# Retention with a state scaled by position: keys on ScalarE, one state sum a tile, gate columns summed by fours

## The chip, the cores and the metric

The kernel runs on one core of one Trainium2 chip. Time is device time in microseconds (us), one execution from start to end. Its engines work side by side, each in the order of its own queue, and wait for each other by semaphores: TensorE (PE, matrix multiplication into PSUM; PEld is its weight load), VectorE (DVE), ScalarE (ACT), GpSimd (POOL), and SyncE (SP), whose queue here starts most DMA transfers.

## The reference, cut to what matters

Three layers in float32: a retention layer, a mixture of experts over its tokens, and a dense MLP with a gated activation. The change touches the first one and the routing columns that are computed from it.

```python
# q, k, v: (8 batches, 8 heads, 576 positions, 64)
gamma = 1.0 - 2.0 ** (-5.0 - np.arange(H))              # one decay for each head
rel = pos[:, None] - pos[None, :]
Dmat = np.where(rel >= 0, gamma[:, None, None] ** rel, 0.0)
ret = (q @ k.T / 8) * Dmat                              # no softmax
x = ret @ v                                             # (4608 tokens, 512)
skip_score = x @ w_skip; logits = x @ w_gate            # 9 columns for the routing
```

## The kernel before

The 4608 tokens are 36 tiles of 128, and nine tiles (`PER`) hold two batches: the tiles tau = 0 to 3 and the first half of tau = 4 are one batch, the second half of tau = 4 and tau = 5 to 8 the other. The kernel has three phases: `phase_a` (retention, routing, and in its gaps the splitting of later weights into two parts), `phase_b` (experts), `phase_c` (the MLP). All instructions are issued in the order in which the Python code calls them; there is no planner. `phase_a` takes the first 244 us, and the change lies in it alone.

Retention goes tile by tile with a running state. For tile t:

- `load` brings q and k (turned, so that the head dimension is on the partitions) and k and v (natural), 1 MB, by SP's queue. The transfer for tile t + 4 goes to the memory of tile t and waits until `mix2(t)` has read it.
- `scores(t)` multiplies k and q of the tile (L403, pairs of heads on two halves of the PE rows), and DVE multiplies the result by the decay matrix into `ret` (L410). Scores have two PSUM buffers, and so has `ret` in SBUF.
- `scale(t)`: POOL multiplies q by gamma^i (`qp`, L384); DVE multiplies k by gamma^(128 - i) (`kp`, L390).
- `state(t)`: 8 matmuls of `kp` and v (L423) give the tile's 64 x 64 state for each head, in the one PSUM buffer `stp`.
- `decay(t)`: POOL multiplies the old state by gamma^128 (`old`, L432). `state_out(t)`: DVE adds the product and `stp` (L444), or copies at a batch's first tile (L442). There are two instructions, for the partition halves, since the state `st` is stored as 128 x 128 blocks for two heads each, with zeros off the diagonal.
- `mix1(t)`: 4 matmuls of `st` of tile t - 1 and `qp` (L458). `mix2(t)`: 8 matmuls of v and `ret` into the same PSUM (L466). ACT copies the sum out as `xT` (L470).
- `rows(t)` turns `xT` back (L480), ACT copies (L482), SP stores. `gate_mm(t)` multiplies `xT` by the nine routing columns in four column groups of PE (L493), ACT copies the result (L496). `gate_turn(t)` turns that (L501), and DVE sums the four parts out of PSUM (L502).

In pass t of the loop the order is: `load(t + 4)`, `state(t)`, `state_out(t)`, `scale(t + 1)`, `decay(t + 1)`, `scores(t + 1)`, `gate_turn(t - 2)`, `mix(t)`, routing of a finished group of four tiles (`route1`, in the next pass `rank`, `slots`, `gates`: some 20 short DVE instructions), `rows(t - 1)`, `gate_mm(t - 1)`, then, in three of four passes, one step of the weight conversion (`conv_step`: L205 to L243, on ACT, DVE and SP). From pass 16 on, an expert weight is split in some passes (L156 on ACT, L159 on DVE). A PE instruction that waits holds up all that is behind it on PE, and so on each engine.

`gate_turn(t - 2)` takes its PSUM from the tag `stp`, which has one buffer and is also that of `state`. So the turn waits until `state_out(t)` has read `stp`, and `state(t + 1)` waits until L502 has read the turned columns. The PSUM tags are `s1` (two buffers of two banks) and `pg`, `stp`, `xT`, `pr` (one bank each).

Of the kernel before, what the change touches and what calls it, by code (L numbers as in the profile page):

```python
# [8 lines left out]
F32 = mybir.dt.float32  # L9
# [10 lines left out]
P = 128  # L20
NT = 36
# [28 lines left out]
C_GQ = C_D + 2 * 1024  # L50
C_GK = C_GQ + 2 * 512
C_GS = C_GK + 8
C_W = C_GS + 4


@with_exitstack
def retention_moe_mlp_kernel(
# [240 lines left out]
    def phase_a():  # L298
        actx = ExitStack()
        with actx:  # L300
# [24 lines left out]
            def dload(eng, off, n):  # L325
# [33 lines left out]
                                    base=0, channel_multiplier=-1)  # L359
            st = [a1.tile([P, KD, P], F32, name=f"st{i}") for i in range(2)]  # L360
            for s in st:
                nc.vector.memset(s, 0.0)
            logits = a1.tile([P, NT, 9], F32, name="logits")
            oh = a1.tile([P, NT + 16, E + 1], BF16, name="oh")
# [10 lines left out]
            qp_t, kp_t, ret_t, xT_t = {}, {}, {}, {}  # L375
            stp = [None, None]

            def scale(t):
                if t >= NT:
                    return  # L380
                tau = t % PER
                if tau != 0:
                    qp = ap.tile([P, 512], F32, tag="qp", name="qp")
                    nc.gpsimd.tensor_tensor(out=qp, in0=in_t[t][:, 0, :],  # L384
                                            in1=dcol(C_GQ + (512 if tau == 4 else 0), 512), op=ALU.mult)
                    qp_t[t] = qp
                if tau != 8:
                    kp = ap.tile([P, E, 64], F32, tag="kp", name="kp")
                    g = dcol(C_GK, 8).unsqueeze(2).to_broadcast([P, E, 64])
                    nc.vector.tensor_tensor(out=kp, in0=in_t[t][:, 2, :].rearrange("p (h d) -> p h d", h=E),  # L390
                                            in1=g, op=ALU.mult)
                    kp_t[t] = kp
# [19 lines left out]

            def state(t):
                tau = t % PER
                if tau == 8:
                    return
                sp = psx.tile([P, KD, 64], F32, tag="stp", name="stp")
                p0 = 64 if tau == 4 else 0
                kp = kp_t.pop(t)
                v = in_t[t][:, 3, :].rearrange("p (h d) -> p h d", h=E)  # L420
                for c in range(KD):
                    for r in range(2):
                        nc.tensor.matmul(out=sp[64 * r:64 * r + 64, c, :], lhsT=kp[p0:, 2 * c + r, :],  # L423
                                         rhs=v[p0:, 2 * c + r, :], start=True, stop=True)
                stp[0] = sp

            def decay(t):

                if t % PER not in (0, 4, 8) and t < NT:
                    g = cst[C_GK][:, 8:12].unsqueeze(2).to_broadcast([P, KD, P])  # L430
                    old = ap.tile([P, KD, P], F32, tag="old", name="old", bufs=1)
                    nc.gpsimd.tensor_tensor(out=old, in0=st[(t - 1) % 2], in1=g, op=ALU.mult)  # L432
                    stp[1] = old

            def state_out(t):
                tau = t % PER
                if tau == 8:
                    return
                for r in range(2):
                    p = slice(64 * r, 64 * r + 64)  # L440
                    if tau in (0, 4):
                        nc.vector.tensor_copy(out=st[t % 2][p, :, p], in_=stp[0][p])  # L442
                    else:
                        nc.vector.tensor_tensor(out=st[t % 2][p, :, p], in0=stp[0][p], in1=stp[1][p, :, p], op=ALU.add)  # L444

# [6 lines left out]
            def mix1(t):  # L452
                tau = t % PER
                x = mix_t[t] = psx.tile([P, KD, P], F32, tag="xT", name="xTp")
                if tau != 0:
                    qp = qp_t.pop(t)
                    for c in range(KD):
                        nc.tensor.matmul(out=x[:, c, :], lhsT=st[(t - 1) % 2][:, c, :],  # L458
                                         rhs=qp[:, c * P:(c + 1) * P], start=c == 0, stop=False)

# [37 lines left out]

            def gate_turn(t, tag="pg", at_once=True):
                pg = psx.tile([P, P], F32, tag=tag, name="pg")  # L500
                nc.tensor.transpose(pg, gs_t.pop(t), ident)  # L501
                add = lambda: nc.vector.tensor_reduce(out=logits[:, t, :],  # L502
                                                      in_=pg.rearrange("p (k c) -> p c k", k=KD)[:, 0:9, :],
# [5 lines left out]
            def route1(ts):  # L509
                t0, n = ts[0], len(ts)  # L510
                sl = slice(t0, t0 + n)
                lg = logits[:, sl, 0:E]
                sh = [P, n, E]
# [8 lines left out]
                eq, am, cm, d = tmp("eq"), tmp("am", [P, n]), tmp("cm", [P, n]), tmp("d")  # L522
                nc.vector.tensor_scalar(out=cm, in0=logits[:, sl, 8], scalar1=0.0, scalar2=None, op0=ALU.is_gt)
                nc.vector.tensor_scalar(out=oh[:, sl, E], in0=cm, scalar1=0.0, scalar2=None, op0=ALU.is_equal)
# [170 lines left out]
            scores(0)  # L695
            for t in range(L):
                if t != 31:
                    load(min(t + 4, 35) if t < 33 else NT)
                if t == 1:
                    conv_load(0)  # L700
                if t == 0:
                    dload(nc.sync, C_D + 1024, 1024)
                    dload(nc.sync, C_GQ + 512, 512)
                if t == 2:
# [16 lines left out]
                scale(t + 1)  # L721
                decay(t + 1)
                scores(t + 1, between=between if ts else None)
# [7 lines left out]
                if t > 1:  # L731
                    gate_turn(t - 2, "stp")
                mix(t)
                slots_e(ts)
                if t - 2 in ends:
                    route1(ends[t - 2])
                    ranks.append(ends[t - 2])
# [11 lines left out]

            pair = GROUPS[-1]  # L750
            gate_turn(L - 3)
            gate_mm(L - 2, "pr")
            scale(L)
            decay(L)
            ret = scores(L, False)
            ts = ranks.pop()
            rank(ts)
            add = gate_turn(L - 2, "stp", False)
            slots(ts)
# [433 lines left out]
def tables():  # L1193
# [8 lines left out]
    for var, m in enumerate((dm, dm * blk[None])):  # L1202

        out[:, C_D + 1024 * var:C_D + 1024 * (var + 1)] = m.reshape(4, 2, P, P).transpose(2, 1, 0, 3).reshape(P, 1024)
    gq = (g[:, None] ** i[None, :]) / 8.0
    for var, m in enumerate((gq, gq * (i < 64)[None])):

        out[:, C_GQ + 512 * var:C_GQ + 512 * (var + 1)] = np.repeat(m.reshape(4, 2, P).transpose(1, 0, 2).reshape(2, 512), 64, 0)
    out[:, C_GK:C_GK + 8] = g[None, :] ** (128.0 - i[:, None])
    out[:, C_GS:C_GS + 4] = np.repeat((g ** 128.0).reshape(4, 2).T, 64, 0)  # L1210
    return out.astype(np.float32)
# [19 lines left out]
```

## Time and profile before

| | us |
|---|---|
| median of 3 runs | 1347.86 (1342.99 to 1348.15) |
| the profiled execution | 1347.85 |
| its span, from the first to the last instruction | 1346.1 |
| share of the span in which PE, DVE, ACT, POOL are busy | 95%, 42%, 30%, 29% |
| mean granted TensorE clock | 0.983 of full speed |

The busy shares of the whole span are those of a PE-bound kernel, but they are means over three phases. The change lies in the first 244 us, so the stretch that counts is that of the loop over the tiles, from 28 to 222 us, which holds 30 tiles. Most of what follows is read in it.

### The profile page before, as it was taken

To read this page: it belongs to the slowest core of one execution; us is meant where nothing else is said; L and a number is where in the kernel's file an instruction comes from. 1 tells how busy PE (TensorE), PEld (TensorE's weight loads), DVE (VectorE), ACT (ScalarE), POOL (GpSimd) and SP (SyncE) were. 2 spreads that over 40 slices of the span, in tenths; PEclk is the share of its full clock that TensorE was granted. 3 is DMA by queue.
4 is the path that set the end of the run, shared out by engine and by line. 5 is a ranking of instruction groups with operands and counts; after the bars stand their busy time and mean duration, and the time that the engine had idled before them with its cause. 6 is when DMAs were issued, how large, how long until landed. Compare 5 with 4: busy or idle time off the path is not lost.

```text
span 1346.1 us, 19306 instructions
## 1 busy us (share of the span) xinstructions
PE 1278.6 (95%) x7682; PEld 1058.3 (79%) x7682; DVE 570.9 (42%) x1037; ACT 410.4 (30%) x708; POOL 386.6 (29%) x332
## 2 busy tenths in 40 slices
PE   8887888899999999999999999999999999999995
PEld 6676666788888888788888888888888888888884
DVE  5988888477887873641111111111111111111111
ACT  2223322444444442332222222222222222222221
POOL 4556445313223221122232222232222222222221
PEclk9989889999999999999999999999999999999998
DMA  9989884547777798430010000000010000000000
GB/s 362 264 235 312 273 291 158 171 145 227 258 237 244 267 317 338 174 102 32 1 44 27 24 32 16 17 32 24 9 39 24 32 16 17 32 0 0 32 0 33
DMA packets 59806, 163.53 MB, mean 121 GB/s; under 512 B 9492, under 2 KB 12564, under 8 KB 53824
## 3 DMA queue, kind: packets, MB, share of 16 engines
q1 hardware_dynamic: 52160, 146.38, 32.6%
q0 software_dynamic: 6592, 15.01, 3.4%
q8 instruction: 62, 1.02, 0.3%
q10 hardware_dynamic: 960, 0.86, 0.2%
q14 instruction: 32, 0.26, 0.1%
HBM read 121.47 MB, written 41.52 MB: 121 GB/s over the span
## 4 chain that ended last, share of the span: by engine, by line
PE 75%; DVE 12%; issue 6%; DMA 4%; POOL 1%; ACT 1%; another core or an unknown queue 0%; POOLq 0%; ACTq 0%; DVEq 0%
PE o L1078 29%; PE ch L1053 27%; PE y L904 6%; PE h L887 5%; DVE ret L410 2%; DMA xd<-xr,ent 1%; PE eh L272 1%; PE cpt L1042 1%; DMA xr<-xd,ent 1%; DVE st L444 1%; PE xTp L466 1%; DVE kp L390 1%; DVE cva L217 1%; PE xTp L458 1%; PE s L403 1%
## 5 line engine op out<-in xcount | busy, mean ns | idle before, releaser
L1053 PE MATMUL ch<-cx,w 128*128 128x512 f32 (+1 forms) x1728 | 398.0, 379 | 3.0 <-DVE gt L1057 3.0
L1078 PE MATMUL o<-w,gh 128*128 128x512 f32 x1120 | 377.7, 398 | 0.0
L1053 PEld LDWEIGHTS ch<-cx,w 128*128 128x128 f32 x1728 | 312.8, 188 | 70.4 <-DVE gt L1057 4.6
L1064 POOL TENSOR_TENSOR gl<-gt,gh 128x512 fp32r<-128x512 f32 (+1 forms) x144 | 178.6, 1240 | 605.2 <-ACT gh L1063 590.1
L1057 DVE SCALAR_TENSOR_TENSOR gt<-r,ch 128x512 f32<-128x512 f32 (+1 forms) x144 | 94.8, 658 | 592.1 <-ACT r L1055 592.1
L1078 PEld LDWEIGHTS o<-w,gh 128*128 128x128 f32 x1120 | 210.6, 188 | 48.1
L1055 ACT ACTIVATE r<-ch,small 128x512 f32<-128x512 f32 (+1 forms) x144 | 95.8, 665 | 435.2 <-PE ch L1053 435.2
L1078 PE MATMUL o<-w,gl 128*128 128x512 f32 x560 | 221.4, 395 | 0.0
L904 PE MATMUL y<-w,hh 128*112 128x512 f32 x384 | 132.4, 400 | 0.0
L887 PE MATMUL h<-x,w 128*128 128x336 f32 x768 | 128.4, 316 | 0.6 <-ACT x L879 0.6
L887 PEld LDWEIGHTS h<-x,w 128*128 128x128 f32 x768 | 122.5, 188 | 6.8 <-ACT x L879 0.8
L1063 ACT CAST gh<-gt 128x512 fp32r<-128x512 f32 (+1 forms) x144 | 86.2, 598 | 134.0 <-DVE gt L1057 133.2
L1078 PEld LDWEIGHTS o<-w,gl 128*128 128x128 f32 x560 | 105.4, 188 | 23.0
L904 PEld LDWEIGHTS y<-w,hh 128*112 128x112 f32 x384 | 67.6, 176 | 18.5
L911 POOL DMA_INDIRECT xd<-xr,ent x24 | 36.3, 1513 | 151.4 <-DVE xr L909 148.1
L159 DVE TENSOR_TENSOR w<-raw,w 128x1024 fp32r<-128x1024 f32 x64 | 78.9, 1235 | 0.0
L904 PE MATMUL y<-w,hl 128*112 128x512 f32 x192 | 75.7, 395 | 0.0
L156 ACT CAST w<-raw 128x1024 fp32r<-128x1024 f32 x64 | 67.0, 1048 | 15.6 <-DMA raw<-in_w_dram 15.5
L470 ACT COPY xT<-xTp 128x512 f32<-128x512 f32 x36 | 21.1, 587 | 154.3 <-PE xTp L466 139.4
L890 ACT ACTIVATE hh<-h 128x336 fp32r<-128x336 f32 x64 | 28.9, 452 | 109.9 <-PE h L887 103.4
L892 DVE SCALAR_TENSOR_TENSOR hl<-h,hh 128x336 fp32r<-128x336 f32 x64 | 32.4, 506 | 46.5 <-ACT hh L890 46.1
L617 POOL DMA_INDIRECT tab<-idt,posi x36 | 37.6, 1045 | 39.6 <-DVE idt L592 17.0
(168 smaller groups left out, 1207.7 us busy)
## 6 DMA issues: line engine op xcount, KB each, us to landing
in<-in_qkv_dram SPq DMA_DIRECT2D x33, 1024.0 KB
raw<-in_w_dram SPq DMA_DIRECT2D x64, 512.0 KB
w<-wsc SPq DMA_DIRECT2D x13, 1024.0 KB
xd<-row SPq DMA_DIRECT2D x36, 256.0 KB
wsc<-cvh SPq DMA_DIRECT2D x18, 512.0 KB
raw<-in_w_in_dram SPq DMA_DIRECT2D x16, 512.0 KB
raw<-in_w_out_dram SPq DMA_DIRECT2D x16, 512.0 KB
cr<-xd SPq DMA_DIRECT2D x31, 256.0 KB
```

Of the source, the lines that this page charges most:

```text
L156: nc.scalar.copy(out=w_tile(i)[:, 0, :], in_=raw_t[i])
L159: nc.vector.tensor_tensor(out=w_t[i][:, 1, :], in0=raw_t.pop(i), in1=w_t[i][:, 0, :].bitcast(F32), op=ALU.subtract)
L617: own_rows("tab", nc.gpsimd.indirect_dma_start(out=tab, out_offset=bass.IndirectOffsetOnAxis(posi[:, t:t + 1], 0), in_=idt2[:, t, :], in_o ...
L887: nc.tensor.matmul(out=h, lhsT=w_t[8 * e + k][:, lw, f * P:(f + 1) * P], rhs=rx[:, k, :], start=n == 0, stop=n == 11)
L904: nc.tensor.matmul(out=y_t[e][t][0:CT, :], lhsT=lg[:, sl], rhs=w[:, rw, :], start=f == 0 and n == 0, stop=f == 7 and n == 2)
L911: own_rows("xd", nc.gpsimd.indirect_dma_start(out=xd, out_offset=bass.IndirectOffsetOnAxis(ent[:, e, t, 0:1], 0), in_=o, in_offset=None, b ...
L1053: nc.tensor.matmul(out=h, lhsT=w_block(f)(k)[:, lw, :], rhs=rx[:, k, :], start=i == 0, stop=i == 11)
L1055: nc.scalar.activation(out=r, in_=h, func=AF.Relu, scale=1.0 / 6.0, bias=bias_half)
L1057: nc.vector.scalar_tensor_tensor(out=gt, in0=r, scalar=1.0, in1=h, op0=ALU.min, op1=ALU.mult)
L1063: nc.scalar.copy(out=gh[:, 0:n], in_=gt)
L1064: nc.gpsimd.tensor_tensor(out=gl[:, 0:n], in0=gt, in1=gh[:, 0:n].bitcast(F32), op=ALU.subtract)
L1078: nc.tensor.matmul(out=o_t[g][t], lhsT=lg[:, sl], rhs=w[:, rw, :], start=f == 0 and n == 0, stop=f == NF - 1 and n == 2)
```

## The change

The state is no longer decayed from tile to tile. Keys are scaled by gamma^(256 - 128 n - i) with n = tau modulo 4, and queries by gamma^(128 n + i - 256) / 8 with n = 1 to 4, so that the powers that belong to the distance of tiles are in the two scales, and the state is a plain sum: st(t) = stp(t) + st(t - 1).

- The POOL product `old` (L432) is gone, and `decay` with it.
- `st` is stored as [128, 4, 64], without zeros. `state_out` is one DVE instruction over 128 partitions, no longer two over 64.
- `mix1` uses 8 matmuls of 64 rows x 64 columns (one for each head), no longer 4 of 128 x 128 with zeros.
- `kp` is written by ACT, head by head: 8 activations (`Copy` with the head's scale from a column of a table), no longer one DVE multiplication of 512 columns.
- `gate_turn` in the loop uses the tag `pg`, and ACT copies the 36 columns to `lg`. DVE sums them once for four tiles (`gate_add`). The last two tiles keep a sum of their own (`gate_turn_add`).
- For tau = 4, POOL scales half of the columns of `qp` and sets the rest to zero.
- The query table has 4 blocks of 512 columns in place of 2, the key table 32 columns in place of 8. Three of the query blocks are loaded by SP in the passes t = 0, 1, 2, ahead of `load(t + 4)`, and the second decay matrix in pass 2 in place of pass 0.

```diff
--- before.py
+++ after.py
...
@@ -357,10 +356,8 @@
             tri = a1.tile([P, P], BF16, name="tri")
             nc.gpsimd.affine_select(out=tri, in_=ones, pattern=[[1, P]], compare_op=ALU.is_gt, fill=0.0,
                                     base=0, channel_multiplier=-1)
-            st = [a1.tile([P, KD, P], F32, name=f"st{i}") for i in range(2)]
-            for s in st:
-                nc.vector.memset(s, 0.0)
-            logits = a1.tile([P, NT, 9], F32, name="logits")
+            st = [a1.tile([P, KD, 64], F32, name=f"st{i}") for i in range(2)]
+            logits = a1.tile([P, 2 * GT, 9], F32, name="logits")
...
             qp_t, kp_t, ret_t, xT_t = {}, {}, {}, {}
-            stp = [None, None]
+            stp = [None]
+
+            def gq(tau):
+                return C_GQ + 512 * ((tau - 1) % 4)
 
             def scale(t):
                 if t >= NT:
@@ -381,14 +381,18 @@
                 tau = t % PER
                 if tau != 0:
                     qp = ap.tile([P, 512], F32, tag="qp", name="qp")
-                    nc.gpsimd.tensor_tensor(out=qp, in0=in_t[t][:, 0, :],
-                                            in1=dcol(C_GQ + (512 if tau == 4 else 0), 512), op=ALU.mult)
+                    n = 64 if tau == 4 else P
+                    cut = lambda x: x.rearrange("p (c i) -> p c i", c=KD)[:, :, 0:n]
+                    nc.gpsimd.tensor_tensor(out=cut(qp), in0=cut(in_t[t][:, 0, :]), in1=cut(dcol(gq(tau), 512)), op=ALU.mult)
+                    if n < P:
+                        nc.gpsimd.memset(qp.rearrange("p (c i) -> p c i", c=KD)[:, :, n:], 0.0)
                     qp_t[t] = qp
                 if tau != 8:
                     kp = ap.tile([P, E, 64], F32, tag="kp", name="kp")
-                    g = dcol(C_GK, 8).unsqueeze(2).to_broadcast([P, E, 64])
-                    nc.vector.tensor_tensor(out=kp, in0=in_t[t][:, 2, :].rearrange("p (h d) -> p h d", h=E),
-                                            in1=g, op=ALU.mult)
+                    n = 8 * (tau % 4)
+                    for h in range(E):
+                        nc.scalar.activation(out=kp[:, h, :], in_=in_t[t][:, 2, 64 * h:64 * h + 64], func=AF.Copy,
+                                             scale=cst[C_GK][:, n + h:n + h + 1])
                     kp_t[t] = kp
 
             def scores(t, at_once=True, between=None):
@@ -411,37 +415,25 @@
                 return lambda: nc.vector.tensor_tensor(out=ret, in0=s, in1=d, op=ALU.mult)
 
             def state(t):
+
                 tau = t % PER
                 if tau == 8:
                     return
-                sp = psx.tile([P, KD, 64], F32, tag="stp", name="stp")
+                stp[0] = psx.tile([P, KD, 64], F32, tag="stp", name="stp")
                 p0 = 64 if tau == 4 else 0
                 kp = kp_t.pop(t)
                 v = in_t[t][:, 3, :].rearrange("p (h d) -> p h d", h=E)
                 for c in range(KD):
                     for r in range(2):
-                        nc.tensor.matmul(out=sp[64 * r:64 * r + 64, c, :], lhsT=kp[p0:, 2 * c + r, :],
+                        nc.tensor.matmul(out=stp[0][64 * r:64 * r + 64, c, :], lhsT=kp[p0:, 2 * c + r, :],
                                          rhs=v[p0:, 2 * c + r, :], start=True, stop=True)
-                stp[0] = sp
-
-            def decay(t):
-
-                if t % PER not in (0, 4, 8) and t < NT:
-                    g = cst[C_GK][:, 8:12].unsqueeze(2).to_broadcast([P, KD, P])
-                    old = ap.tile([P, KD, P], F32, tag="old", name="old", bufs=1)
-                    nc.gpsimd.tensor_tensor(out=old, in0=st[(t - 1) % 2], in1=g, op=ALU.mult)
-                    stp[1] = old
 
             def state_out(t):
                 tau = t % PER
-                if tau == 8:
-                    return
-                for r in range(2):
-                    p = slice(64 * r, 64 * r + 64)
-                    if tau in (0, 4):
-                        nc.vector.tensor_copy(out=st[t % 2][p, :, p], in_=stp[0][p])
-                    else:
-                        nc.vector.tensor_tensor(out=st[t % 2][p, :, p], in0=stp[0][p], in1=stp[1][p, :, p], op=ALU.add)
+                if tau in (0, 4):
+                    nc.vector.tensor_copy(out=st[t % 2], in_=stp[0])
+                elif tau != 8:
+                    nc.vector.tensor_tensor(out=st[t % 2], in0=stp[0], in1=st[(t - 1) % 2], op=ALU.add)
 
             mix_t = {}
 
@@ -455,8 +447,10 @@
                 if tau != 0:
                     qp = qp_t.pop(t)
                     for c in range(KD):
-                        nc.tensor.matmul(out=x[:, c, :], lhsT=st[(t - 1) % 2][:, c, :],
-                                         rhs=qp[:, c * P:(c + 1) * P], start=c == 0, stop=False)
+                        for r in range(2):
+                            p = slice(64 * r, 64 * r + 64)
+                            nc.tensor.matmul(out=x[p, c, :], lhsT=st[(t - 1) % 2][p, c, :],
+                                             rhs=qp[p, c * P:(c + 1) * P], start=c == 0, stop=False)
 
             def mix2(t):
                 tau, x = t % PER, mix_t.pop(t)
@@ -496,10 +490,29 @@
                 nc.scalar.copy(out=gs, in_=pg)
                 gs_t[t] = gs
 
-            def gate_turn(t, tag="pg", at_once=True):
+            lg_t = {}
+
+            def at(t, n):
+                return slice(t % (2 * GT), t % (2 * GT) + n)
+
+            def gate_turn(t):
+
+                pg = psx.tile([P, P], F32, tag="pg", name="pg")
+                nc.tensor.transpose(pg, gs_t.pop(t), ident)
+                g, i = divmod(t, GT)
+                if i == 0:
+                    lg_t[g] = ap.tile([P, GT, KD, 9], F32, tag="lg", name="lg")
+                nc.scalar.copy(out=lg_t[g][:, i], in_=pg.rearrange("p (k c) -> p k c", k=KD)[:, :, 0:9])
+
+            def gate_add(ts):
+                lg = lg_t.pop(ts[0] // GT)[:, 0:len(ts)]
+                nc.vector.tensor_reduce(out=logits[:, at(ts[0], len(ts)), :], in_=lg.rearrange("p t k c -> p t c k"),
+                                        axis=AX.X, op=ALU.add)
+
+            def gate_turn_add(t, tag="pg", at_once=True):
                 pg = psx.tile([P, P], F32, tag=tag, name="pg")
                 nc.tensor.transpose(pg, gs_t.pop(t), ident)
-                add = lambda: nc.vector.tensor_reduce(out=logits[:, t, :],
+                add = lambda: nc.vector.tensor_reduce(out=logits[:, t % (2 * GT), :],
                                                       in_=pg.rearrange("p (k c) -> p c k", k=KD)[:, 0:9, :],
                                                       axis=AX.X, op=ALU.add)
                 return add() if at_once else add
...
@@ -694,13 +707,14 @@
             scale(0)
             scores(0)
             for t in range(L):
+                if t < 3:
+                    dload(nc.sync, gq(t + 2), 512)
+                if t == 2:
+                    dload(nc.sync, C_D + 1024, 1024)
                 if t != 31:
                     load(min(t + 4, 35) if t < 33 else NT)
                 if t == 1:
                     conv_load(0)
-                if t == 0:
-                    dload(nc.sync, C_D + 1024, 1024)
-                    dload(nc.sync, C_GQ + 512, 512)
                 if t == 2:
                     pump_load(1)
                 if t == 3:
...
-                decay(t + 1)
...
                 if t > 1:
-                    gate_turn(t - 2, "stp")
+                    gate_turn(t - 2)
                 mix(t)
                 slots_e(ts)
                 if t - 2 in ends:
+                    gate_add(ends[t - 2])
                     route1(ends[t - 2])
...
-    gq = (g[:, None] ** i[None, :]) / 8.0
-    for var, m in enumerate((gq, gq * (i < 64)[None])):
+    gq = lambda n: g[:, None] ** (128.0 * n + i[None, :] - 256) / 8.0
+    for var, m in enumerate((gq(1), gq(2), gq(3), gq(4))):
 
         out[:, C_GQ + 512 * var:C_GQ + 512 * (var + 1)] = np.repeat(m.reshape(4, 2, P).transpose(1, 0, 2).reshape(2, 512), 64, 0)
-    out[:, C_GK:C_GK + 8] = g[None, :] ** (128.0 - i[:, None])
-    out[:, C_GS:C_GS + 4] = np.repeat((g ** 128.0).reshape(4, 2).T, 64, 0)
+    for n in range(4):
+        out[:, C_GK + 8 * n:C_GK + 8 * n + 8] = g[None, :] ** (256.0 - 128 * n - i[:, None])
     return out.astype(np.float32)
 
 
```

## Rows read from the trace of the kernel before

**Rows 1.** The page: busy time, share of the span and instructions.

```profile
PE 1278.6 (95%) x7682; PEld 1058.3 (79%) x7682; DVE 570.9 (42%) x1037; ACT 410.4 (30%) x708; POOL 386.6 (29%) x332
```

**Rows 2.** Stretches: length, busy time (PE, PEld, DVE, ACT, POOL), clock, DMA share, GB/s.

```profile
15.00:25.00 10.00, 9.55 (x138) 7.85 (x138) 6.10 (x9) 2.61 (x6) 5.53 (x9) 1.00 1.03 419
...
100.00:125.00 25.00, 20.12 (x276) 15.88 (x275) 22.48 (x47) 7.38 (x17) 13.09 (x12) 1.00 0.96 327
...
28.00:222.00 194.00, 161.39 (x2066) 129.25 (x2062) 173.71 (x366) 56.89 (x123) 103.33 (x83) 0.93 0.85 269
```

**Rows 3.** Waits of PE from 28 to 222 us: total, times, longest.

```profile
PE pg L501 <- DVE st L444: 18.3, 11, 3.3
PE pk L565 <- DVE cum L533: 4.2, 4, 1.5
PE pg L501 <- DVE st L442: 3.5, 3, 2.5
...
PE stp L423 <- DVE logits L502: 1.9, 4, 1.0
```

**Rows 4.** Timeline of PE, one tile in which it hardly waits: start, length.

```profile
147.11 0.69 PE L423 MATMUL stp<-in,kp 128*64 128x64 f32 x16
147.73 1.16 PE L403 MATMUL s<-in 64*128 64x128 f32 x16
148.92 0.30 PE L501 MATMUL pg<-ident,gs 128*128 128x128 f32 x1
149.05 1.06 PE L458 MATMUL xTp<-qp,st 128*128 128x128 f32 x8
150.04 1.09 PE L466 MATMUL xTp<-ret,in 128*64 128x128 f32 x16
151.06 0.66 PE L480 MATMUL pr<-ident,xT 128*128 128x128 f32 x4
...
152.01 0.28 PE L423 MATMUL stp<-in,kp 128*64 128x64 f32 x2
```

**Rows 5.** Timeline of PE, a tile in which it waits.

```profile
136.04 0.30 PE L501 MATMUL pg<-ident,gs 128*128 128x128 f32 x1 [2.79 <-DVE st L444]
...
137.16 1.97 PE L466 MATMUL xTp<-ret,in 128*64 128x128 f32 x16
```

**Rows 6.** Timeline of DVE at the same place.

```profile
131.45 1.76 DVE L217 SCALAR_TENSOR_TENSOR cva<-cvb,cva 128x512 f32<-128x512 f32 x1
...
135.05 0.85 DVE L444 TENSOR_TENSOR st<-stp,old 64x256 f32<-64x256 f32 x2
```

**Rows 7.** DVE's groups by line, 28 to 222 us: count, busy us, mean ns.

```profile
L410 DVE TENSOR_TENSOR ret<-s,cst 128x1024 f32<-128x1024 f32 x30 | 36.5, 1217 | 2.6 <-PE xTp L466 1.7 <-PE s L403 0.3
L390 DVE TENSOR_TENSOR kp<-in,cst 128x512 f32<-128x512 f32 x27 | 18.8, 695 | 0.8
L444 DVE TENSOR_TENSOR st<-stp,old 64x256 f32<-64x256 f32 x42 | 17.6, 419 | 7.0 <-PE stp L423 6.7
...
L442 DVE COPY st<-stp 64x256 f32<-64x256 f32 x14 | 5.9, 419 | 3.3 <-PE stp L423 3.2
...
L502 DVE TENSOR_REDUCE logits<-pg 128x9 f32<-128x36 f32 x30 | 5.6, 185 | 0.0
```

**Rows 8.** ACT's groups by line, whole span, those near the new ones.

```profile
L1055 ACT ACTIVATE r<-ch,small 128x512 f32<-128x512 f32 x128 | 88.3, 690 | 425.7 <-PE ch L1053 425.7
...
L205 ACT ACTIVATE cvb<-raw 128x512 f32<-128x512 f32 x32 | 21.8, 682 | 3.9 <-DMA raw<-in_w_out_dram 3.1 <-DMA raw<-in_w_in_dram 0.7
...
L1055 ACT ACTIVATE r<-ch,small 128x256 f32<-128x256 f32 x16 | 7.5, 470 | 9.5 <-PE ch L1053 9.5
```

**Rows 9.** POOL's decay product, 28 to 222 us.

```profile
L432 POOL TENSOR_TENSOR old<-st,cst 128x512 f32<-128x512 f32 x21 | 30.6, 1459 | 45.6 <-DVE st L444 28.5 <-DVE st L442 14.1 <-PE s L403 3.0
```

**Rows 10.** The longest wait for a tile's load, from 15 to 232 us.

```profile
POOL qp L384 <- DMA in<-in_qkv_dram: 2.3, 1, 2.3
```

**Rows 11.** Timeline at the start: the first tile's keys.

```profile
8.12 0.69 DVE L390 TENSOR_TENSOR kp<-in,cst 128x512 f32<-128x512 f32 x1 [4.98 <-DMA cst<-in_consts_dram]
```

## What the change does to the time: the prediction

> **What bounds the kernel now.** The page comes first. Over the whole span PE is busy for 1278.6 of 1346.1 us and DVE for 42% [rows 1]: by these means an edit that saves DVE time would be worth nothing. But the change lies in the tile loop, so the stretches come next. From 28 to 222 us, 30 tiles in 194.0 us (6.47 each), PE is busy 161.4 us and DVE 173.7, which is 90%; the clock is 0.93 and DMA's share 0.85 [rows 2]. So in the loop PE idles 32.6 us and DVE is the fullest engine.
>
> Then PE's waits in that stretch. The largest is the gate turn (L501) for DVE's state sum, 18.3 + 3.5 us; the next tile's state waits 1.9 us for the sum of the gate columns, and the rank matmul 4.2 us for the routing counts [rows 3]. One tile in which PE hardly waits shows what PE needs: from state to state 152.01 - 147.11 = 4.90 us [rows 4]. A tile that waits shows why: the turn starts only when the state sum is done [rows 5], and that sum stands in DVE's queue behind the weight conversion that began at 131.45 [rows 6]. After the wait, `mix2` takes 1.97 us in place of 1.09 [rows 4, 5]; that is nearly twice, as at 1.2 in place of 2.4 GHz.
>
> So in this loop PE and DVE hold each other: the turn and the state share one PSUM buffer, PE can't run ahead of DVE's queue, and each burst of DVE work becomes a gap on PE. Phases B and C start when phase A ends; what the loop saves, the kernel saves.
>
> **The change part by part.** The sum is made against the profiled execution, 1347.85 us (span 1346.1), which stands at the median of the runs, 1347.86.
>
> *The turn moves to another PSUM buffer.* It no longer waits for the state sum: -21.8 us [rows 3]. The state no longer waits for L502: -1.9. What is late next? The new buffer is `pg`, which the gate matmuls use: the turn waits for ACT's copy of the previous gate columns, and `gate_mm(t - 1)` for ACT's new copy `lg`. In the undisturbed tile the turn stands at 148.92 and the gate matmuls come behind `rows`, which begin at 151.06 [rows 4]: 2.1 us for a copy of 36 columns, and ACT is busy only 56.9 of 194 us [rows 2]. I book nothing there. PE still needs the state sum, but only for `state(t + 1)` (the one `stp` buffer) and for `mix1(t + 1)`, most of a tile later, and `ret` and the scores have two buffers. `state(t + 1)` starts 4.9 us after `state(t)` [rows 4], so DVE can be some 4 us late without a gap. Some bursts are longer (a conversion step and a routing group in one pass), so I book +2, between 0 and 10.
>
> *DVE's work.* Keys leave: -18.8 us. The state takes one instruction in place of two; the cost doesn't depend on the partitions as far as 64 x 256 shows, so half of 17.6 + 5.9 goes: -11.8. Thirty sums of 36 columns (5.6) become 8 of 144 columns. Between 0.185 us (36 columns) and 1.217 (1024), on a line, that is 0.30 each: 2.4 us. In all DVE falls by 33.8 to 140.0 us, 4.67 a tile [rows 7]. This is below PE's 4.90, so it is not a term of its own: it is what lets the waits above go.
>
> *ACT's work.* No row shows a 64-column activation with a scale from SBUF. The nearest are L1055, with a bias from SBUF: 690 ns at 512 columns, 470 at 256, on a line 305 at 64 [rows 8]. The bounds are the slope alone, 0.055 us, and a whole 512-column one, 0.69. I take 0.305: 8 x 0.305 = 2.44 us a tile, 65.9 in 27 tiles, and the same for 30 `lg` copies, 9.2. ACT comes to 56.9 + 75.1 = 132 us, 4.40 a tile. The Trainium skill (ScalarE: Activation LUTs, section What ACT_TABLE_LOAD costs) has 186 ns + 0.833 ns a column, and 93 more for an operand by pointer; by it this activation is estimated at 332 ns, and ACT at 138 us. The same page's Rules for kernel authors send multiplications to VectorE and not to ScalarE; no row here shows such a multiplication on ACT.
>
> In ACT's queue the eight keys of tile t + 1 stand ahead of `lg`, `xT(t)`, `row` and `gs`. They wait only for a load and an old buffer. PE wants them 4.9 us later, and `xT` is wanted after `mix2`, 151.06 - 147.11 = 3.95 us into the tile [rows 4]; 2.44 us fit. Cover gone, each 0.1 us more for one activation is 0.8 a tile. At the start there is no cover: the first keys took 0.69 us and the first state waited for them [rows 11]: 2.44 - 0.69 = +1.7.
>
> *PE's work.* `mix1` now issues 8 matmuls, 16 instructions in place of 8. It took 150.04 - 149.05 = 0.99 us. Rows with 16 instructions and 128 columns are `mix2`, 1.02 (two column halves), and the scores, 1.19 (two row halves) [rows 4]. The new form is a mixture of both: I take +0.15, in the 27 tiles that have a `mix1` +4.1 us. The bounds are +0.8 us (as `mix2`) and, if nothing overlaps, 16 at 0.124 = 1.98, +26.7.
>
> *The clock.* At a mean of 0.93 [rows 2], with levels of 1 and a half, 14% of 194 us ran at 1.2 GHz; at the full level that work takes 13.6 us less. Low stretches follow PE's gaps, as in [rows 5]. Two thirds of the gaps go, and I take two thirds: -9, between 0 and -13.6.
>
> *Loads.* The loop moves 269 GB/s x 194 us = 52.2 MB. In 174 us that is 300 GB/s. DMA gave 327 from 100 to 125 us at a share of 0.96, and 419 in a stretch of loads alone [rows 2]. Today's longest late load costs 2.3 us [rows 10]. The tables add 512 KB, 1.3 us of DMA at 419 GB/s. On SP they stand ahead of `load(t + 4)` and wait for nothing, but the last ones are needed within about a tile. For late loads and tables I book +5, between 0 and the whole gain.
>
> *POOL.* The decay product, 30.6 us [rows 9], hangs on the state sum and is off PE's path; I book nothing.
>
> The sum: -21.8 - 1.9 + 2 + 1.7 + 4.1 - 9 + 5 = -19.9, so 1328.0 us; the loop would take 5.8 us a tile.
>
> **The rivals.**
>
> *DMA sets the pace.* At 0.85 of 194 us the DMA engines have 165 us of work [rows 2]. If the share can't rise above about 0.90, the loop takes 183 us: 1337. For it: the share was 0.96 from 100 to 125 us, with little left. Against it: in that row DMA carried 327 GB/s, more than the 300 that the forecast needs.
>
> *The small matmuls don't overlap.* Then `mix1` costs +26.7 and not +4.1: 1328.0 + 22.6 - 5 (loads are not late then) = 1345.6, no change. Against it: halves of rows (L403) and halves of columns (L466) overlap today, 16 in 1.02 to 1.19 us; for it: no row has both at once. The Trainium skill (TensorEngine Tiling (Array Packing), section Key Properties) says that a change of tiling mode drains TensorE; `mix1` now stands in a mode of its own between two others. The undisturbed tile already changes form several times and fits into 4.90 us [rows 4]; no run so far shows the cost of one change alone.
>
> *The wait only moves on*: the change doesn't loosen PE from DVE, since `state(t + 1)` still waits for the sum through `stp`. With DVE at 140 us it would return 33.8 us of work, but if bursts and not the mean hold PE, half of the 21.8 comes back, and with it the clock's 9 halves: 1328.0 + 10.9 + 4.5 = 1343.
>
> *ACT becomes the bound, slower.* Keys stand ahead of `xT` in one queue. ACT has 1.90 us a tile now; with `lg` 2.2. It passes today's 6.47 us when an activation costs (6.47 - 2.2) / 8 = 0.53 us. At the farthest row, 0.69 (0.682 for L205) [rows 8], it is 7.7 us a tile: 37 us more in 30 tiles, 1385. Against it: eight times fewer columns than that row.
>
> **How the numbers follow.** My forecast has 0.62; DMA's pace 0.13, the wait that moves on 0.09, the small matmuls 0.11, ACT 0.05. Runs of this kernel spread over 5 us, so 0.5%, 6.7 us, is about what can be told from no change. The forecast and DMA's pace are faster (0.75), and a little over half of the wait that moves on: 0.80. The rest of that and the small matmuls are within: 0.14. ACT and an unnamed mishap: 0.06. The time is 1328. Below it, no late loads, no residual wait and the full clock make -5 - 2 - 4.6: 1316, and a cheaper `mix1` 1313. Above it the range takes in DMA's pace and reaches the wait that moves on: 1343.
>
> **What would show it.** The turn's wait for the state sum should be gone from PE's waits; from 28 us on a tile should take 5.5 to 6.1 us; the clock in the loop should be above 0.95; `mix1` should take 1.0 to 1.2 us; an activation for the keys 0.25 to 0.35 us, and DVE should fall to some 140 us for 30 tiles. The prediction is wrong if waits for `in` or the tables appear on PE, POOL or ACT, if PE waits for ACT's keys before `state`, or if `mix1` comes near 2 us.

## The result, and the profile after

The changed kernel takes 1323.47 us (median of 4 runs, 1320.12 to 1332.19), the kernel before 1346.74 (4 runs). The ratio is 0.9838, interval 0.9810 to 0.9866: 21.8 us faster by this ratio (23.3 by the two medians), where 19.9 were forecast. The profiled execution is the fastest of the four, 1320.12 us, span 1318.3; some 4 us of its distance from before lie behind phase A, where the change touches nothing.

The same stretch as in [rows 2] (columns as there), and then the 30 tiles themselves, from the start of the fourth `ret` on DVE to that of the 34th:

```profile
28.00:222.00 194.00, 178.20 (x2491) 140.48 (x2488) 141.87 (x357) 119.82 (x391) 87.27 (x79) 0.96 0.89 291
```

```profile
21.20:188.08 166.88, 155.53 (x2244) 120.67 (x2244) 120.07 (x269) 108.17 (x361) 74.44 (x71) 0.96 0.97 320
```

A tile takes 166.88 / 30 = 5.56 us; before, the same 30 tiles took 188.11 (6.27). ACT's busy time has doubled and DVE's is down by a quarter. PE is now the fullest engine, busy for 155.53 of 166.88 us (93%), where before it was DVE with 164.82 of 188.11 (88%). DMA's share is 0.97.

PE's waits, beside [rows 3]:

```profile
PE pk L578 <- DVE cum L546: 3.5, 5, 1.5
PE xTp L452 <- POOL qp L386: 2.9, 1, 2.9
PE s L407 <- DMA in<-in_qkv_dram: 2.1, 2, 1.2
PE pk L577 <- ACT row L476: 1.5, 1, 1.5
...
PE pg L501 <- ACT gs L490: 0.8, 2, 0.5
```

The turn's 21.8 us of waits for the state sum have gone. That is what the prediction said one would see, and the experiments show that it was not the reason. An undisturbed tile on PE, beside [rows 4]:

```profile
97.92 0.69 PE L428 MATMUL stp<-in,kp 128*64 128x64 f32 x16
98.54 1.16 PE L407 MATMUL s<-in 64*128 64x128 f32 x16
...
99.63 0.33 PE L501 MATMUL pg<-ident,gs 128*128 128x128 f32 x1
...
99.89 1.09 PE L452 MATMUL xTp<-qp,st 64*64 64x128 f32 x16
...
100.91 1.09 PE L460 MATMUL xTp<-ret,in 128*64 128x128 f32 x16
101.93 0.66 PE L474 MATMUL pr<-ident,xT 128*128 128x128 f32 x4
```

`mix1` with its 16 instructions takes 100.91 - 99.89 = 1.02 us, as `mix2` does (101.93 - 100.91): the halves overlap. ACT's and DVE's new groups, beside [rows 7, 8] (count, busy us, mean ns):

```profile
L394 ACT ACTIVATE kp<-in,cst 128x64 f32<-128x64 f32 x216 | 54.5, 343 | 0.0
...
L505 ACT COPY lg<-pg 128x36 f32<-128x36 f32 x30 | 5.4, 179 | 6.3 <-PE pg L501 5.2 <-remote 0.9
```

```profile
L436 DVE TENSOR_TENSOR st<-stp,st 128x256 f32<-128x256 f32 x21 | 8.8, 420 | 12.2 <-PE stp L428 12.2
```

The state sum over 128 partitions takes the same 0.42 us as one half did [rows 7].

### The profile page after: what moved, and what is told of

Read it like the earlier page. It is cut to its first block, busy times and chain, and to the rows that moved or that the text cites. A ratio compares the mean times of both kernels' runs of the same rounds, so it can differ in the third digit from the quotient of the medians.

```text
span 1318.3 us, 19928 instructions
## 1 busy us (share of the span) xinstructions
PE 1275.8 (97%) x7938; PEld 1051.0 (80%) x7938; DVE 516.8 (39%) x947; ACT 473.0 (36%) x996; POOL 349.6 (27%) x312
## 4 chain that ended last, share of the span: by engine, by line
PE 67%; issue 7%; DMA 5%; DVE 2%; POOL 2%; ACT 0%; POOLq 0%; SPq 0%; DVEq 0%; ACTq 0%
PE o L1091 30%; PE ch L1066 28%; PE y L917 4%; PE h L900 3%; DMA xd<-xr,ent 3%; DMA xr<-xd,ent 1%; PE cpt L1055 1%; PE eh L271 1%; POOL xr L876 1%; POOL xd L924 1%; PE pt L890 0%; DVE cva L208 0%; DMA raw<-in_w_in_dram 0%; DVE xr L922 0%; DMA gse<-ge 0%
## 5 line engine op out<-in xcount | busy, mean ns | idle before, releaser
L1077 POOL TENSOR_TENSOR gl<-gt,gh 128x512 fp32r<-128x512 f32 (+1 forms) x144 | 178.1, 1237 | 605.6 <-ACT gh L1076 600.6
L394 ACT ACTIVATE kp<-in,cst 128x64 f32<-128x64 f32 x256 | 64.6, 342 | 0.0
L386 POOL TENSOR_TENSOR qp<-in,cst 128x512 f32<-128x512 f32 (+1 forms) x32 | 41.2, 1289 | 55.1 <-DMA in<-in_qkv_dram 16.6
L414 DVE TENSOR_TENSOR ret<-s,cst 128x1024 f32<-128x1024 f32 x35 | 42.6, 1217 | 25.9 <-PE s L407 13.7
```

The source lines that it names most:

```text
L394: nc.scalar.activation(out=kp[:, h, :], in_=in_t[t][:, 2, 64 * h:64 * h + 64], func=AF.Copy, scale=cst[C_GK][:, n + h:n + h + 1])
L1077: nc.gpsimd.tensor_tensor(out=gl[:, 0:n], in0=gt, in1=gh[:, 0:n].bitcast(F32), op=ALU.subtract)
```

## The experiments

Gains are given as the ratio to the kernel before, timed on the same chip; the kernel before took 1339 us there for e1 to e8 and 1348 for e9 to e12. A difference between two experiments is a difference of such ratios, and both intervals count in it. The first four take the change apart. Theory A is the prediction's: the PSUM buffer that the turn and the state share ties PE to DVE's queue. Theory B: the amount of DVE's work is what counts.

**e1_turn_alone**: the kernel before with the gate columns as in the changed one.

```diff
-                    gate_turn(t - 2, "stp")
+                    gate_turn(t - 2)
...
+                    gate_add(ends[t - 2])
                     route1(ends[t - 2])
```

> The kernel before with one part of the change: the gate turn in the PSUM tag pg, ACT's copy lg, one sum for four tiles. Keys stay on DVE, the state decays on POOL. Theory A (the shared PSUM buffer ties PE to DVE's queue): PE's 21.8 us of waits of the turn for the state sum mostly go and the kernel gains 8 to 16 us. Theory B (DVE's amount of work is what holds the loop; DVE keeps about 170 of 194 us): no gain, within 4 us.

Ratio 1.0033 (1.0013 to 1.0052): no gain, some 4 us slower. PE's waits from 28 to 222 us:

```profile
PE pk L584 <- DVE cum L552: 13.6, 6, 3.9
PE stp L423 <- DVE kp L390: 7.8, 5, 4.1
PE xTp L458 <- POOL qp L384: 3.2, 1, 3.2
PE pk L583 <- ACT row L482: 1.8, 1, 1.8
```

The turn waits no more, and PE waits instead for two other products of the same DVE queue: the routing counts and the keys, 13.6 + 7.8 us where the turn had 21.8.

**e2_sum_alone**: the changed kernel with the keys on DVE and the gate turn as before.

```diff
-                    for h in range(E):
-                        nc.scalar.activation(out=kp[:, h, :], in_=in_t[t][:, 2, 64 * h:64 * h + 64], func=AF.Copy,
-                                             scale=cst[C_GK][:, n + h:n + h + 1])
+                    g = cst[C_GK][:, n:n + 8].unsqueeze(2).to_broadcast([P, E, 64])
+                    nc.vector.tensor_tensor(out=kp, in0=in_t[t][:, 2, :].rearrange("p (h d) -> p h d", h=E),
+                                            in1=g, op=ALU.mult)
...
-                    gate_turn(t - 2)
+                    gate_turn_add(t - 2, "stp")
...
-                    gate_add(ends[t - 2])
```

> The changed kernel with keys on DVE and the gate turn as before (tag stp, a DVE sum for each tile): what is left is the state scaled by position, one sum a tile, no product on POOL, the small matmuls. Theory A: 0 to 5 us faster than before, the turn still waits for the state sum some 15 us or more in the loop. Theory B: DVE loses 12 us of work, so 8 to 12 us faster.

Ratio 0.9836 (0.9819 to 0.9854): the whole gain, without the turn and without ACT. The turn still shares its buffer with the state, and yet PE's waits for it have shrunk from 18.3 and 3.5 us [rows 3] to 6.1 and 1.9:

```profile
PE pg L514 <- DVE st L436: 6.1, 7, 1.6
...
PE pg L514 <- DVE st L434: 1.9, 3, 1.0
```

**e3_turn_as_before**: the changed kernel with only the second part of that edit (the turn as before, keys on ACT).

```diff
-                    gate_turn(t - 2)
+                    gate_turn_add(t - 2, "stp")
...
-                    gate_add(ends[t - 2])
```

> The changed kernel with the gate turn alone as before (tag stp, a DVE sum for each tile); keys on ACT. Theory A: most of the gain is lost, 3 to 10 us faster than before. Theory B: DVE is down by 30 us all the same, so 15 to 20 us faster than before.

Ratio 0.9876 (0.9854 to 0.9897).

**e4_keys_dve**: the changed kernel with only the first part (keys on DVE, the turn as changed), the lines on `kp` in the diff of e2.

> The changed kernel with the keys on DVE, one multiplication of 512 columns a tile. DVE has 18.8 us more, ACT 56 us less. Theory A: 12 to 18 us faster than before, since PE no longer stands behind each burst. Theory B: 8 to 12 us faster, half of the gain.

Ratio 0.9852 (0.9835 to 0.9868).

Theory A falls: the turn alone gives nothing, and without it the gain stays, or nearly (e3). Theory B is right on what counts, but not in size: e2 saves 12 us of DVE instructions and gains 22, and in e4, which came out 20 us faster, above A's figure too, the keys' 18.8 us on DVE cost nothing that can be told from noise. A third theory, C, was formed: DVE's time for a tile is the pace, and besides the second state instruction POOL's decay product costs DVE time, by stretching its instructions. Its rival D: the product was a brake as a link of the chain, since the sum waits for it.

**e5_two_sums**: e2 with the state sum in two halves.

```diff
-                    nc.vector.tensor_tensor(out=st[t % 2], in0=stp[0], in1=st[(t - 1) % 2], op=ALU.add)
+                for p in (slice(0, 64), slice(64, 128)):
...
+                        nc.vector.tensor_tensor(out=st[t % 2][p], in0=stp[0][p], in1=st[(t - 1) % 2][p], op=ALU.add)
```

> The kernel of e2 (position-scaled sum, keys and gate sums as before) with the state sum in two DVE instructions of 64 partitions, as before. Theory C (DVE's time per tile sets the loop: one instruction less and no stretching by POOL's product): 27 more instructions of 0.42 us, some 12 us, come back, so 8 to 12 us faster than before. Theory D (the product's place in a chain over POOL was the brake): the whole gain of e2, 18 to 22 us, stays.

Ratio 0.9922 (0.9894 to 0.9950): 0.0086 of 1339 us, 11.5 us, come back (some 7 to 16 by the two intervals), as C says.

**e6_idle_product**: e2 with a product on POOL that nobody waits for.

```diff
                 scale(t + 1)
+                if (t + 1) % PER not in (0, 4, 8):
+                    g = cst[C_GK][:, 8:12].unsqueeze(2).to_broadcast([P, KD, P])
+                    idle = ap.tile([P, KD, P], BF16, tag="old", name="old", bufs=1)
+                    nc.gpsimd.tensor_tensor(out=idle, in0=dcol(C_D, 512).rearrange("p (c i) -> p c i", c=KD), in1=g, op=ALU.mult)
```

> The kernel of e2 plus a product of 512 columns a tile on POOL that nobody waits for: its inputs are constants and its output (bf16, for want of room) is read by no one. Theory C: DVE's instructions that share ports with POOL get longer again, 3 to 8 us come back. Theory D: without the chain no more than 2 us come back.

Ratio 0.9946 (0.9927 to 0.9965): 14.7 us come back (some 11 to 18), nearly twice the upper figure of C and far from D. DVE's groups from 28 to 190 us, first of e2, then of e6:

```profile
L414 DVE TENSOR_TENSOR ret<-s,cst 128x1024 f32<-128x1024 f32 x30 | 36.4, 1212 | 9.2 <-PE xTp L460 3.8 <-DMA cst<-in_consts_dram 3.7 <-PE s L407 1.3
L394 DVE TENSOR_TENSOR kp<-in,cst 128x512 f32<-128x512 f32 x26 | 18.9, 727 | 0.0
...
L436 DVE TENSOR_TENSOR st<-stp,st 128x256 f32<-128x256 f32 x19 | 7.9, 418 | 6.9 <-PE stp L428 6.9
...
L208 DVE SCALAR_TENSOR_TENSOR cva<-raw,cva 128x512 int32<-128x512 int32 x8 | 6.0, 747 | 0.3
...
L219 DVE TENSOR_SCALAR cvb<-cva 128x512 int32<-128x512 int32 x7 | 3.1, 440 | 0.2
```

```profile
L414 DVE TENSOR_TENSOR ret<-s,cst 128x1024 f32<-128x1024 f32 x27 | 32.7, 1212 | 8.7 <-DMA cst<-in_consts_dram 4.0 <-PE xTp L460 3.3 <-PE s L407 1.3
L394 DVE TENSOR_TENSOR kp<-in,cst 128x512 f32<-128x512 f32 x23 | 19.6, 851 | 0.0
L208 DVE SCALAR_TENSOR_TENSOR cva<-raw,cva 128x512 int32<-128x512 int32 x7 | 8.5, 1218 | 0.2
...
L436 DVE TENSOR_TENSOR st<-stp,st 128x256 f32<-128x256 f32 x17 | 7.1, 419 | 8.1 <-PE stp L428 8.1
...
L219 DVE TENSOR_SCALAR cvb<-cva 128x512 int32<-128x512 int32 x7 | 4.7, 673 | 0.2
```

Instructions that read both operands from SBUF are longer on average with the product (keys 727 to 851 ns, the masking step L208 747 to 1218); those that read one from PSUM, `ret` and the state sum, are the same to within a nanosecond. Some with a single operand, in SBUF, are longer too (L219, 440 to 673), and not every line moved that way (L221, with two, went from 1163 to 1031). The means come from a few long instructions: L208's median is 693 ns, and one takes 3.36 us. The Trainium skill (SBUF — State Buffer, section SBUF: two separate sides) says that VectorE and GpSimd share one port pair, held for a whole instruction, and that a VectorE instruction needs it when it has two SBUF inputs and the GpSimd one reads SBUF, or when it runs in a two-port mode. The keys and L208 agree; no run here shows the mode of L219.

Beside the long one of L208 POOL ran the query product and, directly behind it, the idle one:

```profile
127.41 3.36 DVE L208 SCALAR_TENSOR_TENSOR cva<-raw,cva 128x512 int32<-128x512 int32 x1
```

```profile
127.94 1.28 POOL L386 TENSOR_TENSOR qp<-in,cst 128x512 f32<-128x512 f32 x1
129.16 1.04 POOL L739 TENSOR_TENSOR old<-cst,cst 128x512 bf16<-128x512 f32 x1
```

**e7_compact_decay**: the kernel before with the compact state alone; the product stays in the chain, half as wide.

```diff
-            st = [a1.tile([P, KD, P], F32, name=f"st{i}") for i in range(2)]
+            st = [a1.tile([P, KD, 64], F32, name=f"st{i}") for i in range(2)]
...
+                    nc.vector.tensor_tensor(out=st[t % 2], in0=stp[0], in1=stp[1], op=ALU.add)
```

> The kernel before with the compact state alone: 64 columns a head, one state sum in place of two, the small matmuls; the decay product stays on POOL and in the chain, over 256 columns in place of 512. Keys, queries and gate turn as before. Theory C: 10 to 16 us faster than before. Theory D: no more than 4 us faster.

Ratio 0.9892 (0.9868 to 0.9916), 14.5 us faster, with the chain over POOL kept, though with a shorter product in it. With e5 and e6, D falls as the main cause.

The 30 tiles in the kernels so far and in e11, which comes next (length of the stretch and DVE's busy time in it, from one profile each):

| kernel | 30 tiles, us | DVE busy, us | difference | ratio to before |
|---|---|---|---|---|
| before | 188.1 | 164.8 | 23.3 | 1 |
| e1 turn alone | 191.5 | 165.0 | 26.4 | 1.0033 |
| e6 sum, idle product | 182.0 | 155.6 | 26.4 | 0.9946 |
| e5 sum in two | 178.1 | 155.9 | 22.2 | 0.9922 |
| e7 compact, decay kept | 170.6 | 144.5 | 26.0 | 0.9892 |
| e2 sum alone | 168.3 | 142.2 | 26.1 | 0.9836 |
| e4 keys on DVE | 162.9 | 135.7 | 27.1 | 0.9852 |
| e11 changed, sum in two | 165.8 | 131.4 | 34.4 | 0.9834 |
| e3 turn as before | 167.0 | 125.9 | 41.1 | 0.9876 |
| changed | 166.9 | 120.1 | 46.8 | 0.9838 |

Three of these rows as the profile gives them, of before, e2 and e6:

```profile
19.89:208.00 188.11, 157.59 (x2028) 126.22 (x2027) 164.82 (x347) 56.26 (x120) 100.39 (x86) 0.94 0.88 283
```

```profile
19.35:187.66 168.31, 152.89 (x2244) 119.45 (x2244) 142.22 (x320) 55.40 (x120) 77.31 (x72) 0.98 0.95 319
```

```profile
20.58:202.61 182.03, 157.59 (x2246) 122.56 (x2247) 155.63 (x320) 55.54 (x120) 100.39 (x93) 0.95 0.90 294
```

Down to some 136 us of DVE work the stretch is DVE's busy time plus 22 to 27 us; below that it stays at 163 to 168, whatever DVE has to do. Between e2 and e6 DVE has the same 320 instructions and 13.4 us more busy time. Between before and e2 it falls by 22.6 us, with 347 - 320 = 27 instructions fewer: these are 27 x 0.42 = 11.3 us. The lengths of all the others, added up, fall by 8.3 us; the rest, some 3 us, is that the records of neighbours overlap more.

**e11_two_sums_after**: the changed kernel with e5's edit, the same lines, to test that floor.

> The changed kernel with the state sum in two DVE instructions of 64 partitions: the edit that cost some 11 us in the kernel of e5. Theory C with a floor (the loop takes DVE's time plus some 11 us until DVE falls to about 155 us for 30 tiles, then PE's own need): DVE has 129 us here, 141 with the edit, so nothing, within 3 us of the changed kernel. If DVE's time counts still: 8 to 12 us slower.

Ratio 0.9834 (0.9796 to 0.9872), as the changed kernel: the edit that cost 11.5 us above the floor is free on it, though DVE's time rose from 120.1 to 131.4. The kernel also differs from e5's by the keys and the turn's buffer. That in e5 the longer sum counted through DVE's time, and not as a link in PE's path to the turn, is argued from e1, where the turn left that path and the loop stayed at DVE's time plus 26 us; it was not tested by itself.

**e12_scores_twice**: the changed kernel with each score matmul done twice.

```diff
-                    for r in range(2):
+                    for r in (0, 1, 0, 1):
                         nc.tensor.matmul(out=s[:, r, c, :], lhsT=a[64 * r:64 * r + 64, 1, c, :],
```

> The changed kernel with each score matmul done twice (the same data to the same place): PE has 1.2 us more a tile, 42 us in 35 tiles at the full clock, DVE and ACT nothing more. If PE is the floor of the loop now: 30 to 42 us slower than the changed kernel. If DMA or a chain over ACT is: 5 to 20 us slower.

Ratio 0.9971 (0.9943 to 0.9999), 18 us slower than the changed kernel. The added work was less than expected: the scores take 81.57 - 79.59 = 1.98 us a tile in place of 99.63 - 98.54 = 1.09, so 31 us in 35 tiles. The scores and the 30 tiles:

```profile
79.59 2.06 PE L407 MATMUL s<-in 64*128 64x128 f32 x32
81.57 0.33 PE L501 MATMUL pg<-ident,gs 128*128 128x128 f32 x1
```

```profile
24.52:205.90 181.38, 176.03 (x2724) 143.69 (x2724) 122.27 (x270) 109.89 (x362) 74.18 (x70) 1.00 0.88 292
```

PE is now busy for 97% at the full clock, and more than half of the added work lengthens the loop, 14.5 of 26.7 us. The rest went into idle time (11.4 us in the changed kernel, 5.4 here) and into the clock, which is 1.00 here and was 0.96. By the ranges of the expectation 18 us belongs to the rivals, DMA or a chain over ACT. DMA is answered by e8, and ACT by e4, where it has 61 us of work and the 30 tiles take 4 us less. That PE with its remaining small waits is the larger part of the floor is therefore argued, and it is not all of it.

**e8_more_dma**: the changed kernel with one more transfer a tile.

```diff
+                if 3 < t < 34:
+                    off = gq(t % PER + 3)
+                    nc.sync.dma_start(out=cst[off], in_=consts[:, off:off + 512])
```

> The changed kernel plus one transfer of 256 KB a tile for 30 tiles (a query table is loaded once more, the same data, at a time when nobody uses it): 7.9 MB, 19 to 25 us of all DMA engines at 312 to 419 GB/s. If DMA, now at a share of 0.95, sets the loop's pace: 15 us slower than the changed kernel, that is 2 to 8 us faster than before. If PE sets it and the loads have slack: within 5 us of the changed kernel.

Ratio 0.9883 (0.9856 to 0.9909), 6 us slower than the changed kernel (some 1 to 11 by the two intervals) for 7.9 MB, between the two expectations. DMA moves 345 GB/s in its 30 tiles, where the changed kernel had 320. PE's first wait from 28 to 190 us is now for a load:

```profile
PE s L407 <- DMA in<-in_qkv_dram: 6.1, 3, 3.4
```

DMA does not set the pace, but its slack is small: about two thirds of the added transfer time was hidden.

**e9_row3** and **e10_keys_dve_row3**: in the changed kernel ACT waits for a row's store before it can copy the next row (4.9 us from 20 to 200 us; 9.0 in e4), and keys stand behind it. Both kernels have three row buffers, the second also has the keys on DVE.

```diff
-                row = ap.tile([P, D], F32, tag="row", name="row")
+                row = ap.tile([P, D], F32, tag="row", name="row", bufs=3)
```

> The changed kernel with three row buffers in place of two (to make room, some small tiles have one buffer in place of two). In the changed kernel ACT waits some 8 to 10 us for a row's store before it can write the next row, and keys, xT and gate columns stand behind it. If that is what keeps the loop above PE's own need: 3 to 8 us faster than the changed kernel. If the stores are late because DMA as a whole is late, or the wait falls where PE has slack: within 2 us.

> The kernel of e4 (keys on DVE, all else as changed) with three row buffers. Same two theories: 3 to 8 us faster than e4, or within 2 us of it. If keys on ACT cost the loop something, it is the fastest of all.

Ratios 0.9827 (0.9791 to 0.9863) and 0.9802 (0.9762 to 0.9842). ACT's waits for the stores are gone from the first one's list, and its 30 tiles take 166.1 us, as before that edit: the wait fell where PE had slack. The second takes 162.7 us for them, as e4 its 162.9. It is the fastest by its middle value, but its interval takes in the changed kernel's 0.9838; no version was shown to beat it.

## Why the prediction was right, and where it was not

The time, 1328 against 1323.5, and the side were right. The mechanism was wrong in its largest step, and the total came out by luck: two errors in the split, a term that gave nothing and one that was booked at nothing, have nearly the same size.

- *The turn's PSUM buffer, -21.8.* This step failed. Done alone (e1) it gives nothing; left out (e3) it is missed by some 5 us, with intervals that overlap and 30 tiles that take the same 167 us. The wait was read off the trace correctly, but a wait names the instruction at which PE meets DVE's backlog, not the price of the meeting. With DVE busy for 165 of 188 us PE meets the same backlog one instruction later.
- *DVE's work, "not a term of its own", and POOL, nothing.* These two were the term. The prediction did say that DVE's fall "lets the waits above go", but it booked the gain on the buffer. The second state instruction is 11.5 us (e5). The rest of e2's 22 came when the product left: e5, with two sums and no product (and with the compact state and the small matmuls), is 10.4 us faster than before, and DVE is busy for 155.9 us in place of 164.8. By DVE's fall of 33.8 us the 30 tiles should have had 131 us of DVE work; they have 120.
- *How the product cost DVE time* is shown in part. The 1.76 us of [rows 6] is an instruction that the profile of e2 shows at 0.74 on average (L216), so the stretching stood in the trace of before. But beside it on POOL ran the query product (L384), which the changed kernel keeps, and not the decay product (L432):

```profile
128.44 1.50 POOL L432 TENSOR_TENSOR old<-st,cst 128x512 f32<-128x512 f32 x1
...
131.12 1.55 POOL L384 TENSOR_TENSOR qp<-in,cst 128x512 f32<-128x512 f32 x1
```

Counting what each DVE instruction takes beyond the shortest of its line (from 60 ns on), the 30 tiles of before have 27.5 us, 23.8 of it beside the query product alone and 1.3 beside the decay product alone; e2 has 20.0 and e5 18.3, nearly all beside the query product. So the real product hardly held DVE up itself. In e6 it is different: the idle product stands directly behind the query product, and 23.2 of 34.2 us are instructions that met both. So e6 shows that a product on POOL can cost this much, and its 14.7 us are not the price of the one that was removed. How that one, waiting for the state sum in POOL's queue, led the query products to meet more of DVE's long instructions stays open.

- *Keys on ACT.* 343 ns each, and eight start to end in 2.02 us, where 2.44 were booked: 0.25 us for each, one behind the other. The Trainium skill (ScalarE: Activation LUTs, section What ACT_TABLE_LOAD costs) gives an estimated 332 ns by its sum and an overlap of about 93 between neighbours; the row and the timeline agree. The move earns nothing: on the floor DVE's time is free (e4).

```profile
57.70 2.02 ACT L394 ACTIVATE kp<-in,cst 128x64 f32<-128x64 f32 x8
```

- *Small matmuls, +4.1.* 1.02 us, +0.03 a tile, the lower bound; the rival that they don't overlap falls. No cost of the change of form is to be seen.
- *The clock, -9.* The mean in the loop rose from 0.93 to 0.96 (from 0.94 in the 30 tiles), less than two thirds of the way. Both levels are still in the rows of the changed kernel: beside the 1.09 us above, the same `mix2` takes 1.97 us in another tile, as in [rows 5]. There the granted clock is 0.50 (1.2 GHz) from 65.85 to 71.30 us, after PE was busy for 1.6 of 3.8 us.

```profile
69.31 1.97 PE L460 MATMUL xTp<-ret,in 128*64 128x128 f32 x16
```

- *Late loads, +5, and the start, +1.7.* Waits for loads on PE are 2.1 us from 28 to 222 us. The fourth state starts 2.2 us later than before.
- *The rivals.* "DMA sets the pace" is refused by e8, and the share, which that rival had stopping at 0.90, rose to 0.97; but it was nearer than the other rivals. "The wait only moves on" is what the turn does by itself; that its room was given by DVE's lost work, and not by the buffer, was the point that I didn't see. ACT is at 108 of 167 us and no bound.

What stays open: which part of the floor of 163 to 168 us belongs to which of PE's remaining waits. The largest are for the routing counts (3.5 us) and once for POOL's query product (2.9), and in e12 about half of the added PE work counted; a saving was not tried.

## What to carry to other kernels

When one engine is busy for most of a stretch (here DVE, for 88%), a wait for it may be its backlog showing: price a change by the busy time that it takes off that engine, and then look where the next engine's floor lies. Moving the wait to another buffer was worth nothing here. Count on that engine's account also what others do to the length of its instructions: compare the mean of one instruction with its shortest, and look at which instruction of another engine ran beside the long ones, before you name the one that cost it. A single edit tried alone and left out alone tells more than the list of waits.

## What the runs showed of the hardware

In e6 a product on GpSimd that nobody waits for, 22 of 1.14 us each in the 30 tiles, cost the kernel 14.7 us and added 13.4 us to VectorE's busy time in these tiles. It lengthened VectorE instructions with both operands in SBUF, and some with a single one there, and left those with one in PSUM alone; an instruction whose median is 0.69 us took 3.36 us where the query product and the idle one ran beside it, one directly behind the other. A state sum on VectorE takes 0.42 us over 64 as over 128 partitions. TensorE instructions of 64 rows by 64 columns on opposite halves of rows and columns overlap as well as those on column halves: 16 with 128 columns in 1.02 us.
